# Attention scores in tiles of 64 keys by 72 queries, with TensorE's order written out

## The chip, the cores and the metric

The kernel runs on one core of one Trainium2 chip. The metric is the device time of one execution in microseconds (us). Before the change the median of 10 executions is 1340.0 us (1339.74 to 1340.58).

A core has a matrix engine (TensorE, "PE" in the profile, with its weight loads listed apart as "PEld"), a vector engine (VectorE, "DVE"), a scalar engine that evaluates functions (ScalarE, "ACT"), GpSimd ("POOL") and a queue that issues transfers (SyncE, "SP"). They work at the same time, each on its own list of instructions, and wait for each other through semaphores. A matmul takes its two operands from the on-chip memory SBUF and writes into PSUM, from which ScalarE or VectorE must read the result before the buffer can be used again.

## The reference, cut to what matters

S = 2048 tokens, D = 1024, 32 heads of 32, a window of 8 keys at a distance of 2 tokens, F = 3584:

```python
for layer in range(2):
    # A: sliding, dilated attention
    q, k, v = split_heads(layernorm(layernorm(x)) @ wqkv)
    idx    = pos[:, None] - 2 * arange(8)[None, :]           # each query sees 8 keys
    logits = where(idx >= 0, (q . k[idx]) * 32 ** -0.5, -1e9)
    o      = softmax(logits) . v[idx]
    x      = x + o @ wo
    # B: token-mixing MLP
    h = layernorm(layernorm(x))
    x = x + transpose(gelu(transpose(h) @ w1 + b1) @ w2 + b2)
```

(The doubled layernorm is the call's own and the block's.)

## The kernel before, in words

The tokens are kept in two classes, even (c = 0) and odd (c = 1), because the window steps by two: inside a class of 1024 tokens a query sees its own key and the seven before it. Tokens are taken in blocks of 128, eight to a class.

A layer has these stages, one after another on TensorE: the value projection (`v_proj`, L216); the attention loop; the output projection (`out_proj`, L311), which also adds the residual and makes the next layernorm; the MLP's first product (`gemm1`, L337) and its second (`gemm2`, L380).

**The attention loop** goes over 16 units u = (g, c): a group g of four heads, which fills 128 rows, and a class c. In unit u three kinds of work meet on TensorE:

- *Dense work*: `qk_chunk` (L228) projects q and k of unit u + 1. Unit u + 1 has four chunks (q or k, first or second 512 tokens), each of eight 128x128 by 512 matmuls (L233) into an `m` buffer, of which there are two; VectorE moves each result to SBUF (L236). In a layer's last unit the first four `out_proj` calls stand in their place.
- *Scores*: `scores(u, r)` (L238), three times in a unit, for three, three and two blocks of 128 keys. For each block and each head there is one matmul (L248): 32 rows (the head's own 32 rows of the array), 128 keys as columns, 136 queries streamed. The 136 are the block's own 128 and the 8 that follow, which still see its last keys. The four heads write into four PSUM banks, two `s` buffers of two banks each, all that there are of `s`. ScalarE takes the exponential into `Pm` (L252), VectorE multiplies in place by the 0/1 pattern `band` (L255), in each case once for two heads.
- *Values*: `values(u, b)` (L257), for each half of the class (b = 0, 1): products of `Pm` with v in tiles of 128 rows by 32 columns (L269, L273), sums of `Pm` over keys (L277, L285), all in the one `acc` buffer. ScalarE turns the sums into their reciprocals as exp(-ln) (L288, L289), and VectorE multiplies (L291).

`Pm` exists twice and is used by units in turn. The loop at L434 calls, for each unit: `scores(u, 0)`, chunk, `values(u - 1, 1)`, `scores(u, 1)`, chunk, `scores(u, 2)`, chunk, `values(u, 0)`, chunk.

**What sets the order.** The program names engines and buffers; a planner walks the instructions with a cost model, takes the earliest in the program's order among those that it reckons to be ready, assigns buffers from the pools as they come free, and writes each engine's list with the semaphore waits. So an engine's list is close to the order of the calls but need not be equal to it; where the planner reckons that an operand or a buffer is not there yet, it puts later work ahead. On the chip the list is then run in its order. `rd`, the reciprocals' buffer, has a pool of two; `xr`, `xn`, `xs` and `xo` (rows of the residual stream) share the pool `x2p` of five.

At the start GpSimd makes the constants (the identity, `band`), clears the padding of `qT` (L146) and requests the two bias transfers (L136, L137), whose results VectorE converts (L138, L139), while VectorE also makes the first layernorms (L169 to L177) that the value projection needs.

Of the kernel before, what the change touches and what calls it, by code (L numbers as in the profile page):

```python
# [14 lines left out]
P = 128  # L15
H = 32
DH = 32
# [8 lines left out]
def kernel(  # L26
# [33 lines left out]
    KW = P + W  # L60
    PAD = W
# [13 lines left out]
    x2p = pool("x2p", 5)  # L75
    rdp = pool("rdp", 2)
# [32 lines left out]
    def ln_exp_table():  # L109
# [13 lines left out]
    band = const.tile([P, KW], BF16, name="band")  # L123
    nc.gpsimd.memset(band[:], 1.0)
    nc.gpsimd.affine_select(out=band[:], in_=band[:], compare_op=ALU.is_ge, fill=0.0, base=0,
                            pattern=[[1, KW]], channel_multiplier=-1)
    nc.gpsimd.affine_select(out=band[:], in_=band[:], compare_op=ALU.is_ge, fill=0.0, base=W - 1,
                            pattern=[[-1, KW]], channel_multiplier=1)
# [16 lines left out]
    for t in qT:  # L145
        nc.gpsimd.memset(t[:, S:S + PAD], 0.0)  # L146

# [80 lines left out]
    def qk_chunk(u, wts, part, n):  # L228
        g, c = divmod(u, DIL)
        ps = m_tile()  # L230
        lo = c * SC + n * 512
        for kt in range(KD):
            nc.tensor.matmul(ps[:], lhsT=wts[part][:, kt, (g % 2) * P:(g % 2 + 1) * P], rhs=hT[:, kt, lo:lo + 512],  # L233
                             start=(kt == 0), stop=(kt == KD - 1))
        dst = (qT, kT)[part][g % 2]
        nc.vector.tensor_copy(out=dst[:, lo:lo + 512], in_=ps[:])  # L236

    def scores(u, r):  # L238
        g, c = divmod(u, DIL)
        q, k, pm = qT[g % 2], kT[g % 2], Pm[u % 2]  # L240
        ts = range(3 * r, min(3 * r + 3, NI))
        n = len(ts)
        ss = [s_tile() for _ in range(2)]
        for t in ts:
            lo = c * SC + t * P
            for h in range(HG):
                hp = slice(h * DH, (h + 1) * DH)
                nc.tensor.matmul(ss[h // 2][:, h % 2, (t - ts[0]) * KW:(t - ts[0] + 1) * KW],  # L248
                                 lhsT=k[hp, lo:lo + P], rhs=q[hp, lo:lo + KW], start=True, stop=True)
        for b in range(2):  # L250
            pv = pm[:, 2 * b:2 * b + 2, ts[0]:ts[0] + n, :]
            nc.scalar.activation(out=pv.rearrange("p h t k -> p h (t k)"), in_=ss[b][:, :, 0:n * KW], func=ACT.Exp,  # L252
                                 scale=scale, bias=shift[:])
            mk = band[:].unsqueeze(1).unsqueeze(1).to_broadcast([P, 2, n, KW])
            nc.vector.tensor_tensor(out=pv, in0=pv, in1=mk, op=ALU.mult)  # L255

    def values(u, b, v, oT):  # L257
# [24 lines left out]
        for h in range(HG):  # L282
            hp = slice(h * DH, (h + 1) * DH)
            dst = acc[hp, 1, :].rearrange("p (t q) -> p t q", q=P)[:, o0 // P:o0 // P + ns, 0:W]
            nc.tensor.matmul(dst, lhsT=ones[:], rhs=pm[:, h, s0:s0 + ns, P:KW], start=False, stop=True,  # L285
                             skip_group_check=True)
        rd = rdp.tile([P, 512], FP32, name="rd", tag="rd")
# [3 lines left out]
        nc.vector.tensor_tensor(out=oT[g][:, lo:lo + hb * P], in0=acc[:, 0, :], in1=rd[:], op=ALU.mult)  # L291

# [10 lines left out]
    def out_proj(c, i, oT, wo, res, dst, h2):  # L303
        xr = x2("xr")
        nc.sync.dma_start(out=xr[:], in_=res(c, i))
        xn = x2("xn")
        for n in range(NDC):
            ps = m_tile()
            xs_ = slice(n * 512, (n + 1) * 512)
            for g in range(NG):  # L310
                nc.tensor.matmul(ps[:], lhsT=oT[g][:, cols(c, i)], rhs=wo[n][g // 4][:, g % 4, :],  # L311
                                 start=(g == 0), stop=(g == NG - 1))
# [4 lines left out]
        norm_act(h2[c][i][:], xn[:], mean, rs)  # L317

# [73 lines left out]
    for li in range(2):  # L392
# [41 lines left out]
        for u in range(NU):  # L434
            last = u == NU - 1
            if not last:
                if (u + 1) % (2 * DIL) == 0:
                    wts = load_qk((u + 1) // (2 * DIL))
                fill = [lambda part=part, n=n: qk_chunk(u + 1, wts, part, n) for part, n in chunks]
            else:  # L440
                fill = [lambda i=i: out_proj(0, i, oT, wo, res, xa[li], h2) for i in range(4)]
            if u == NU - 2:
                wo = load_wo()
            scores(u, 0)
            fill[0]()
            if u:
                values(u - 1, 1, v, oT)
            scores(u, 1)
            fill[1]()
            scores(u, 2)  # L450
            fill[2]()
            values(u, 0, v, oT)
            fill[3]()
        values(NU - 1, 1, v, oT)
# [41 lines left out]
```

## Time and profile before

| | |
|---|---|
| median of 10 executions | 1340.0 us |
| the profiled execution's own time | 1339.83 us |
| its span, first to last instruction | 1338.1 us |
| TensorE busy | 1313.1 us, 98% of the span |
| VectorE busy | 428.2 us, 32% |
| ScalarE busy | 407.0 us, 30% |
| GpSimd busy | 4.0 us |
| dense q and k matmuls (L233) | 1024, 247.0 us |
| score matmuls (L248) | 1024, 41.0 us |
| value matmuls (L273) of 136 columns | 768, 22.7 us |
| attention loop, layer 1 | 81.3 to 248.3 us |
| attention loop, layer 2 | 738.8 to 905.8 us |

How to read the rows. In an order of time: start, length, engine, line, operation, output and inputs by the program's names, shape, count of merged instructions, and in brackets the idle time of that engine before the row with what ended it. In groups: line, engine, operation, shape and count, then total busy time and mean nanoseconds of one, then the idle time ahead of them. In windows: the stretch and its length, then busy time and count for PE, PEld, DVE, ACT and POOL, then TensorE's granted clock as a share, the DMA engines' share and GB/s. Matmuls overlap and their ends are modelled, so the distance between starts is the surer measure of what one costs. "m", "s" and "acc" are the three kinds of PSUM buffers.

### The profile page before, as it was taken

The numbers are of one execution on the slowest core, as the hardware profiler recorded it, in microseconds if no ns is written. First come the engines' busy times: TensorE is split into PE (matmuls) and PEld (weight loads), VectorE is DVE, ScalarE is ACT, GpSimd is POOL, SyncE is SP. The second block draws the span as 40 slices with busy tenths as digits, with TensorE's granted clock in tenths as the row PEclk, the third lists the DMA queues.
The fourth block names the chain that finished last, engine by engine and source line by source line (L and its number), as shares of the span: only waits on it lengthen the run. The fifth ranks groups of instructions, "written<-read, shape, count | busy, mean of one in ns | idle before, by whom it ended". The sixth has DMA issues, their size and how long they took to land.

```text
span 1338.1 us, 19150 instructions
## 1 busy us (share of the span) xinstructions
PE 1313.1 (98%) x8352; PEld 590.7 (44%) x8352; DVE 428.2 (32%) x774; ACT 407.0 (30%) x622; POOL 4.0 (0%) x13
## 2 busy tenths in 40 slices
PE   6999999999999999999999999999999999999998
PEld 3444444444444444444444444444444444444443
DVE  6146666960000013233210667678300000011111
ACT  4347766542111110000023677675311111000000
POOL 1000000000000000000000000000000000000000
PEclk8999999999999999999999999999999999999999
DMA  9521110462222226546431101124522221334420
GB/s 251 119 64 33 33 33 28 143 193 79 63 79 77 64 70 163 129 127 182 118 95 47 35 17 33 32 75 154 151 79 79 71 81 56 119 94 124 132 89 32
DMA packets 192195, 121.83 MB, mean 91 GB/s; under 512 B 34416, under 2 KB 173680, under 8 KB 192112
## 3 DMA queue, kind: packets, MB, share of 16 engines
q1 hardware_dynamic: 192000, 120.61, 32.2%
q8 instruction: 65, 1.06, 0.3%
q0 software_dynamic: 112, 0.01, 0.1%
q14 instruction: 18, 0.15, 0.0%
HBM read 96.48 MB, written 16.78 MB: 85 GB/s over the span
## 4 chain that ended last, share of the span: by engine, by line
PE 92%; ACT 6%; DMA 1%; issue 0%; DVE 0%; SPq 0%
PE s L380 14%; PE s L337 14%; PE m L233 13%; PE m L311 8%; PE m L216 8%; PE m L380 7%; PE acc L337 7%; PE m L337 7%; PE acc L380 7%; ACT Pm L252 3%; PE s L248 1%; PE acc L273 1%; ACT rd L289 1%; ACT rd L288 1%; PE acc L277 1%; DMA x<-in_A_x_dram 1%
## 5 line engine op out<-in xcount | busy, mean ns | idle before, releaser
L380 PEld LDWEIGHTS <-w 128*128 128x128 bf16 x1792 | 175.4, 98 | 211.4
L337 PEld LDWEIGHTS <-w 128*128 128x128 bf16 x1792 | 175.3, 98 | 211.5
L233 PE MATMUL m<-hT,wqk 128*128 128x512 bf16 x1024 | 247.0, 381 | 0.0
L337 PE MATMUL s<-h,w 128*128 128x512 bf16 x896 | 202.8, 379 | 0.0
L380 PE MATMUL s<-g,w 128*128 128x512 bf16 x896 | 199.9, 379 | 0.0
L383 DVE SCALAR_TENSOR_TENSOR xo<-s,b_sb,xs 128x512 bf16<-128x512 f32 x32 | 24.0, 750 | 540.7 <-PE s L380 536.5
L252 ACT ACTIVATE Pm<-s,shift 128x816 bf16<-128x816 f32 (+1 forms) x192 | 152.3, 861 | 39.6 <-PE s L248 39.6
L233 PEld LDWEIGHTS <-wqk 128*128 128x128 bf16 x1024 | 90.3, 98 | 109.2 <-issue 6.6
L216 PE MATMUL m<-wv,hT 128*128 128x512 bf16 x512 | 113.9, 385 | 5.5 <-ACT hT L199 5.5
L311 PE MATMUL m<-wo,oT 128*128 128x512 bf16 x512 | 112.2, 379 | 0.0
L255 DVE TENSOR_TENSOR Pm<-Pm,band 128x816 bf16<-128x816 bf16 (+1 forms) x192 | 99.9, 532 | 29.7 <-ACT Pm L252 25.1
L337 PE MATMUL acc<-h,w 128*128 128x512 bf16 x448 | 103.9, 379 | 0.0
L380 PE MATMUL acc<-g,w 128*128 128x512 bf16 x448 | 100.6, 379 | 0.0
L380 PE MATMUL m<-g,w 128*128 128x512 bf16 x448 | 99.3, 379 | 0.0
L337 PE MATMUL m<-h,w 128*128 128x512 bf16 x448 | 99.0, 379 | 0.0
L163 ACT ACTIVATE ln<-mv,eps 128x1 f32<-128x1 f32 x64 | 18.7, 293 | 236.7 <-DVE mv L171 236.5
L344 ACT ACTIVATE g<-s,b_sb 128x1024 bf16<-128x1024 f32 x28 | 31.2, 1114 | 166.9 <-PE s L337 166.9
L216 PEld LDWEIGHTS <-hT 128*128 128x128 bf16 x512 | 50.4, 99 | 67.7 <-ACT hT L199 6.1
L236 DVE CAST qT<-m 128x512 bf16<-128x512 f32 x64 | 44.0, 687 | 100.2 <-PE m L233 100.1
L311 PEld LDWEIGHTS <-oT 128*128 128x128 bf16 x512 | 49.3, 98 | 59.6 <-issue 0.9
L291 DVE TENSOR_TENSOR oT<-acc,rd 128x512 bf16<-128x512 f32 x64 | 44.3, 692 | 59.0 <-ACT rd L289 58.9
L288 ACT ACTIVATE rd<-acc 128x512 f32<-128x512 f32 x64 | 38.2, 597 | 66.6 <-PE acc L285 66.6
(50 smaller groups left out, 585.7 us busy)
## 6 DMA issues: line engine op xcount, KB each, us to landing
w<-in_B_w_dram SPq DMA_DIRECT2D x56, 512.0 KB, 3.7
w<-in_B_w_dram SPq DMA_DIRECT2D x64, 448.0 KB, 4.3
wqk<-in_A_wqkv_dram SPq DMA_DIRECT2D x16, 512.0 KB, 5.4
xa<-xn SPq DMA_DIRECT2D x32, 256.0 KB, 2.1
xs<-xa SPq DMA_DIRECT2D x32, 256.0 KB, 3.0
x<-in_A_x_dram SPq DMA_DIRECT2D x16, 256.0 KB, 6.6
wv<-in_A_wqkv_dram SPq DMA_DIRECT2D x8, 512.0 KB, 5.7
xr<-in_A_x_dram SPq DMA_DIRECT2D x16, 256.0 KB, 3.1
```

The source lines that it names most:

```text
L216: nc.tensor.matmul(ps[:], lhsT=hT[:, kt, cols(c, i)], rhs=wv[n][kt // 4][:, kt % 4, :], start=(kt == 0), stop=(kt == KD - 1))
L233: nc.tensor.matmul(ps[:], lhsT=wts[part][:, kt, (g % 2) * P:(g % 2 + 1) * P], rhs=hT[:, kt, lo:lo + 512], start=(kt == 0), stop=(kt == KD ...
L236: nc.vector.tensor_copy(out=dst[:, lo:lo + 512], in_=ps[:])
L252: nc.scalar.activation(out=pv.rearrange("p h t k -> p h (t k)"), in_=ss[b][:, :, 0:n * KW], func=ACT.Exp, scale=scale, bias=shift[:])
L255: nc.vector.tensor_tensor(out=pv, in0=pv, in1=mk, op=ALU.mult)
L288: nc.scalar.activation(out=rd[:], in_=acc[:, 1, :], func=ACT.Ln)
L291: nc.vector.tensor_tensor(out=oT[g][:, lo:lo + hb * P], in0=acc[:, 0, :], in1=rd[:], op=ALU.mult)
L311: nc.tensor.matmul(ps[:], lhsT=oT[g][:, cols(c, i)], rhs=wo[n][g // 4][:, g % 4, :], start=(g == 0), stop=(g == NG - 1))
L337: nc.tensor.matmul(pairs[fl][0][dc], lhsT=wt[c][:, i, fl * P:(fl + 1) * P], rhs=h2[c][i][:, dc * 512:(dc + 1) * 512], start=(k == 0), stop ...
L344: nc.scalar.activation(out=g[fb][:, fl, :].rearrange("p (n d) -> p n d", n=2), in_=t[:], func=ACT.Gelu_apprx_tanh, bias=b1_sb[:, ft:ft + 1])
L380: nc.tensor.matmul(aps[dc], lhsT=w2t[ft // HF][:, ft % HF, c::DIL], rhs=g[ft // GF][:, ft % GF, dc * 512:(dc + 1) * 512], start=(ft == 0), ...
L383: nc.vector.scalar_tensor_tensor(out=xo[:, dc * 512:(dc + 1) * 512], in0=aps[dc], scalar=b2_sb[:, i, c:c + 1], in1=xs[:, dc * 512:(dc + 1) ...
```

## The change

- *Score tiles.* A block of 128 keys is taken in two halves r of 64 keys. A half is multiplied with its own 64 queries and the 8 after them: 72 columns streamed instead of 136, and an output of 64 PSUM partitions. A matmul is now 32 rows by 64 columns of the array, so that eight places stand side by side instead of four, and there are twice as many score matmuls, each with its own weight load.
- *Exponential and mask.* `scores(u, b)` is called twice in a unit, for four blocks each. ScalarE takes the exponential of the compact form (4 heads x 4 blocks x 72) into a new tile `pc`, two buffers, in two instructions; VectorE multiplies by `band` (now two copies of a 64-row pattern) and writes into the dense `Pm`, once for each half on 64 partitions. The two corners of each `Pm` block that no half writes are cleared once, at the start, by GpSimd.
- *Order.* `in_order` hangs each call's TensorE instructions behind the last matmul of the call before, so the planner cannot change TensorE's order inside the loop. The loop runs over 32 visits (u, b): scores, chunk, the values of the visit before, chunk. The chunks come as q, q, k, k.
- *Copies.* The chunk of the first 512 tokens (n = 0) is moved to SBUF by ScalarE, the other by VectorE.
- *Buffers and transfers.* `rd` moves into `x2p`, which grows to six; `wo` is requested six visits from the end instead of two units from the end.

```diff
-    x2p = pool("x2p", 5)
-    rdp = pool("rdp", 2)
+    x2p = pool("x2p", 6)
+    pcp = pool("pcp", 2)
...
-    band = const.tile([P, KW], BF16, name="band")
+    band = const.tile([P, HW], BF16, name="band")
...
+    for r in range(2):
+        hb_ = band[r * HK:(r + 1) * HK]
+        nc.gpsimd.affine_select(out=hb_, in_=hb_, compare_op=ALU.is_ge, fill=0.0, base=0,
+                                pattern=[[1, HW]], channel_multiplier=-1)
...
+    for t in Pm:
+        nc.gpsimd.memset(t[0:HK, :, :, HW:KW], 0.0)
+        nc.gpsimd.memset(t[HK:P, :, :, 0:HK], 0.0)
...
-        nc.vector.tensor_copy(out=dst[:, lo:lo + 512], in_=ps[:])
+        if n == 0:
+            nc.scalar.copy(out=dst[:, lo:lo + 512], in_=ps[:])
+        else:
+            nc.vector.tensor_copy(out=dst[:, lo:lo + 512], in_=ps[:])
+        return mm
+
+    last_pe = [None]
+
+    def in_order(f, *args):
+        with tc.issue_after(last_pe[0].ins) if last_pe[0] is not None else nullcontext():
+            last_pe[0] = f(*args)
+
+    HB = NI // 2
 
-    def scores(u, r):
+    def scores(u, b):
         g, c = divmod(u, DIL)
         q, k, pm = qT[g % 2], kT[g % 2], Pm[u % 2]
-        ts = range(3 * r, min(3 * r + 3, NI))
-        n = len(ts)
         ss = [s_tile() for _ in range(2)]
-        for t in ts:
-            lo = c * SC + t * P
-            for h in range(HG):
-                hp = slice(h * DH, (h + 1) * DH)
-                nc.tensor.matmul(ss[h // 2][:, h % 2, (t - ts[0]) * KW:(t - ts[0] + 1) * KW],
-                                 lhsT=k[hp, lo:lo + P], rhs=q[hp, lo:lo + KW], start=True, stop=True)
-        for b in range(2):
-            pv = pm[:, 2 * b:2 * b + 2, ts[0]:ts[0] + n, :]
-            nc.scalar.activation(out=pv.rearrange("p h t k -> p h (t k)"), in_=ss[b][:, :, 0:n * KW], func=ACT.Exp,
-                                 scale=scale, bias=shift[:])
-            mk = band[:].unsqueeze(1).unsqueeze(1).to_broadcast([P, 2, n, KW])
-            nc.vector.tensor_tensor(out=pv, in0=pv, in1=mk, op=ALU.mult)
+        for i in range(HB):
+            for r in range(2):
+                lo = c * SC + (b * HB + i) * P + r * HK
+                for h in range(HG):
+                    hp = slice(h * DH, (h + 1) * DH)
+                    mm = nc.tensor.matmul(ss[h // 2][r * HK:(r + 1) * HK, h % 2, i * HW:(i + 1) * HW],
+                                          lhsT=k[hp, lo:lo + HK], rhs=q[hp, lo:lo + HW], start=True, stop=True)
+        pc = pcp.tile([P, HG, HB, HW], BF16, name="pc", tag="pc")
+        for n in range(2):
+            nc.scalar.activation(out=pc[:, 2 * n:2 * n + 2].rearrange("p h t k -> p h (t k)"), in_=ss[n][:, :, 0:HB * HW],
+                                 func=ACT.Exp, scale=scale, bias=shift[:])
+        for r in range(2):
+            rp = slice(r * HK, (r + 1) * HK)
+            mk = band[rp].unsqueeze(1).unsqueeze(1).to_broadcast([HK, HG, HB, HW])
+            nc.vector.tensor_tensor(out=pm[rp, :, b * HB:(b + 1) * HB, r * HK:r * HK + HW], in0=pc[rp], in1=mk, op=ALU.mult)
+        return mm
...
-        rd = rdp.tile([P, 512], FP32, name="rd", tag="rd")
+        rd = x2("rd", [P, 512], FP32)
...
-        chunks = [(0, 0), (1, 0), (0, 1), (1, 1)]
+        chunks = [(0, 0), (0, 1), (1, 0), (1, 1)]
+        last_pe[0] = None
         for part, n in chunks:
-            qk_chunk(0, wts, part, n)
+            in_order(qk_chunk, 0, wts, part, n)
...
+        for vis in range(2 * NU):
+            u, b = divmod(vis, 2)
+            if b == 0 and u + 1 < NU and (u + 1) % (2 * DIL) == 0:
+                wts = load_qk((u + 1) // (2 * DIL))
+            if vis == 2 * NU - 6:
                 wo = load_wo()
-            scores(u, 0)
...
+            in_order(scores, u, b)
+            for n in range(2):
+                if n and vis:
+                    in_order(values, *divmod(vis - 1, 2), v, oT)
+                if u + 1 < NU:
+                    in_order(qk_chunk, u + 1, wts, *chunks[2 * b + n])
+                else:
+                    in_order(out_proj, 0, 2 * b + n, oT, wo, res, xa[li], h2)
+        in_order(values, NU - 1, 1, v, oT)
```

Here P = 128, W = 8, HK = 64, KW = 136 and HW = 72; `values` and `out_proj` now return their last matmul and are otherwise as they were.

More of the change, by code (lines that the diff above doesn't have):

```diff
@@ L60 @@
     KW = P + W
+    HK = P // 2
+    HW = HK + W
     PAD = W
@@ L232, in qk_chunk @@
         for kt in range(KD):
-            nc.tensor.matmul(ps[:], lhsT=wts[part][:, kt, (g % 2) * P:(g % 2 + 1) * P], rhs=hT[:, kt, lo:lo + 512],
-                             start=(kt == 0), stop=(kt == KD - 1))
+            mm = nc.tensor.matmul(ps[:], lhsT=wts[part][:, kt, (g % 2) * P:(g % 2 + 1) * P], rhs=hT[:, kt, lo:lo + 512],
+                                  start=(kt == 0), stop=(kt == KD - 1))
         dst = (qT, kT)[part][g % 2]
-        nc.vector.tensor_copy(out=dst[:, lo:lo + 512], in_=ps[:])
@@ L284, in values @@
             dst = acc[hp, 1, :].rearrange("p (t q) -> p t q", q=P)[:, o0 // P:o0 // P + ns, 0:W]
-            nc.tensor.matmul(dst, lhsT=ones[:], rhs=pm[:, h, s0:s0 + ns, P:KW], start=False, stop=True,
-                             skip_group_check=True)
-        rd = rdp.tile([P, 512], FP32, name="rd", tag="rd")
+            mm = nc.tensor.matmul(dst, lhsT=ones[:], rhs=pm[:, h, s0:s0 + ns, P:KW], start=False, stop=True,
+                                  skip_group_check=True)
+        rd = x2("rd", [P, 512], FP32)
         nc.scalar.activation(out=rd[:], in_=acc[:, 1, :], func=ACT.Ln)
@@ L291, in values @@
         nc.vector.tensor_tensor(out=oT[g][:, lo:lo + hb * P], in0=acc[:, 0, :], in1=rd[:], op=ALU.mult)
+        return mm
     def load_wo():
@@ L310, in out_proj @@
             for g in range(NG):
-                nc.tensor.matmul(ps[:], lhsT=oT[g][:, cols(c, i)], rhs=wo[n][g // 4][:, g % 4, :],
-                                 start=(g == 0), stop=(g == NG - 1))
+                mm = nc.tensor.matmul(ps[:], lhsT=oT[g][:, cols(c, i)], rhs=wo[n][g // 4][:, g % 4, :],
+                                      start=(g == 0), stop=(g == NG - 1))
             nc.vector.tensor_tensor(out=xn[:, xs_], in0=ps[:], in1=xr[:, xs_], op=ALU.add)
@@ L317, in out_proj @@
         norm_act(h2[c][i][:], xn[:], mean, rs)
+        return mm
     order = [(c, i) for c in range(DIL) for i in range(NI)]
```

25 lines of the change are left out of this document (2 added, 23 removed).

## The prediction

> **What bounds the kernel now.** I read the page's engine shares first, then three windows, then one unit of the attention loop in order of time, then single instants of it for start times.
>
> ```profile
> span 1338.1 us, 19150 instructions
> PE 1313.1 (98%) x8352; PEld 590.7 (44%) x8352; DVE 428.2 (32%) x774; ACT 407.0 (30%) x622; POOL 4.0 (0%) x13
> 81.33:90.19 8.86, 8.86 (x90) 3.76 (x90) 6.11 (x11) 6.09 (x8) 0.00 (x0) 1.00 0.01 2
> 100.28:110.37 10.09, 9.79 (x117) 4.29 (x118) 6.91 (x13) 7.10 (x10) 0.00 (x0) 1.00 0.10 32
> ```
>
> The profiled execution took 1339.83 us, 1.73 around its span; the median is 1340.0. TensorE is the bound, at full clock (the 1.00 after the five engines). A unit u takes 10.09 us and, in 100.28 to 110.37, holds 6.91 us of VectorE and 7.10 of ScalarE. Units 1 to 14 of each layer are alike; unit 0 (8.86) lacks one values block, and the last has out_proj in place of the projection. The change touches only these 32 units. One of them, TensorE's rows:
>
> ```profile
> 110.37 0.36 PE L248 MATMUL s<-qT,kT 32*128 32x136 bf16 x12
> 110.66 1.90 PE L233 MATMUL m<-hT,wqk 128*128 128x512 bf16 x8
> 110.77 1.77 ACT L252 ACTIVATE Pm<-s,shift 128x816 bf16<-128x816 f32 x2 [0.83 <-PE s L248]
> ...
> 112.49 0.19 PE L269 MATMUL acc<-Pm,v 128*32 128x8 bf16 x4
> 112.50 0.25 PEld L273 LDWEIGHTS <-v 128*32 128x32 bf16 x16
> 112.53 0.40 PE L273 MATMUL acc<-Pm,v 128*32 128x136 bf16 x16
> ...
> 112.98 0.19 PE L285 MATMUL acc<-Pm,ones 128*32 128x32 bf16 x4
> ...
> 113.10 0.36 PE L248 MATMUL s<-qT,kT 32*128 32x136 bf16 x12
> ...
> 113.39 1.90 PE L233 MATMUL m<-hT,wqk 128*128 128x512 bf16 x8
> ...
> 115.38 0.30 PE L248 MATMUL s<-qT,kT 32*128 32x136 bf16 x4
> ...
> 115.61 0.39 PE L233 MATMUL m<-hT,wqk 128*128 128x512 bf16 x1
> ...
> 116.21 0.29 PE L248 MATMUL s<-qT,kT 32*128 32x136 bf16 x4 [0.21 <-ACT Pm L252]
> ...
> 116.44 1.68 PE L233 MATMUL m<-hT,wqk 128*128 128x512 bf16 x7
> ...
> 118.05 0.42 PE L273 MATMUL acc<-Pm,v 128*32 128x136 bf16 x16
> ...
> 118.63 1.90 PE L233 MATMUL m<-hT,wqk 128*128 128x512 bf16 x8
> ...
> 120.46 0.35 PE L248 MATMUL s<-qT,kT 32*128 32x136 bf16 x10
> ```
>
> A row's length includes the modelled tail of its last matmul, so I go from start to start. A chunk of eight dense matmuls holds the array 110.66 to 112.49 = 1.83 us. Its own pace is (1.90 - 0.39) / 7 = 0.216 each, 1.73 for eight, so leaving a chunk for small tiles costs 0.10. Values take 0.61 (112.49 to 113.10) and 0.58 (118.05 to 118.63). A score piece of twelve takes 0.29 (110.37 to 110.66). The third piece is broken in two around one dense matmul and waits: its chunk began at 113.39 and would end at 115.22, but the scores start at 115.38; the lone matmul from 115.61 would give way at 115.61 + 0.216 + 0.10 = 115.93, but the next start is 116.21. That is 0.16 + 0.28 = 0.44 us of waiting, and the releaser named is the exponential, ACT Pm.
>
> **The change, part by part.** Each unit becomes two visits: scores (S), a chunk, values, a chunk. Dense matmuls, values and the total of dense work stay. So a new unit is 4 x 1.83 + 0.61 + 0.58 + 2 x S = 8.51 + 2 x S, where S runs from the first score matmul to the first dense one.
>
> S is the unknown: 32 pairs of load and matmul, 32 rows by 64 keys by 72 queries, eight places in the array. No row has this shape. The nearest ones (the first is one instant inside the twelve, with the twelfth alone left):
>
> ```profile
> 110.51 0.22 PE L248 MATMUL s<-qT,kT 32*128 32x136 bf16 x1
> ...
> 112.99 0.18 PE L285 MATMUL acc<-Pm,ones 128*32 128x32 bf16 x1
> ```
>
> - Tail: the last score matmul starts at 110.51, dense work at 110.66: 0.15 us with 136 columns. At 0.216 / 512 = 0.42 ns a column, 64 columns fewer are 0.03 less: 0.12.
> - Spread within a round: four L285 in different places start within 0.19 - 0.18 = 0.01 us, about 3.3 ns apart; eight of them 0.025.
> - A round of eight cannot be shorter than its matmul (72 x 0.42 = 0.03) nor, likely, than its load: at 112.50 the loads of 32 columns start and at 112.53 the matmuls that need them. So 0.027 for 32 columns (an estimate, the rows round), 0.055 for 64.
>
> Four rounds are three intervals: 3 x 0.055 + 0.025 + 0.12 = 0.31 us. Low end, loads hidden too: 3 x 0.03 + 0.025 + 0.12 = 0.24. High end, eight places worth no more than the four of today's twelve, which start (0.36 - 0.22) / 11 = 12.7 ns apart: 31 x 0.0127 + 0.12 = 0.51. I take 0.31, since the load is what the row at 112.53 shows waiting.
>
> Then a steady unit is 9.13 instead of 10.09: 0.96 saved, made of 0.44 waiting, one switch out of dense work of five (0.10), and shorter scores. Fourteen give 13.44. Unit 0: 8.86 against 4 x 1.83 + 0.58 + 0.62 = 8.52, saves 0.34. The last unit: score pieces of 0.29 + 0.29 + 0.23 (115.38 to 115.61) become 0.62, saves 0.19. A layer 13.97, two layers 27.9. On the profiled time: 1339.83 - 27.9 = 1311.9, and with the 0.17 between that run and the median, 1312.
>
> **What the other engines get.** They must stay hidden under a visit of 4.57 us.
>
> ```profile
> L252 ACT ACTIVATE Pm<-s,shift 128x816 bf16<-128x816 f32 x128 | 113.1, 933 | 39.0 <-PE s L248 39.0
> L255 DVE TENSOR_TENSOR Pm<-Pm,band 128x816 bf16<-128x816 bf16 x128 | 74.3, 581 | 28.9 <-ACT Pm L252 25.1
> L291 DVE TENSOR_TENSOR oT<-acc,rd 128x512 bf16<-128x512 f32 x64 | 44.3, 692 | 59.0 <-ACT rd L289 58.9
> L236 DVE CAST qT<-m 128x512 bf16<-128x512 f32 x64 | 44.0, 687 | 100.2 <-PE m L233 100.1
> L252 ACT ACTIVATE Pm<-s,shift 128x544 bf16<-128x544 f32 x64 | 42.2, 716 | 0.7 <-PE s L248 0.7
> L289 ACT ACTIVATE rd<-rd 128x512 f32<-128x512 f32 x64 | 40.3, 630 | 2.1
> L288 ACT ACTIVATE rd<-acc 128x512 f32<-128x512 f32 x64 | 38.2, 597 | 66.6 <-PE acc L285 66.6
> L218 ACT CAST v<-m 128x512 bf16<-128x512 f32 x64 | 37.4, 585 | 61.6 <-PE m L216 61.5
> L255 DVE TENSOR_TENSOR Pm<-Pm,band 128x544 bf16<-128x544 bf16 x64 | 27.9, 435 | 0.7
> ```
>
> - Exponentials: (933 - 716) / 272 = 0.80 ns an element; 576 elements cost 742 ns. ScalarE per visit: 2 x 0.742 + a copy of 0.585 + 0.597 + 0.630 = 3.30.
> - Masks: (581 - 435) / 272 = 0.54 ns; 1152 elements on half the partitions cost 0.76. VectorE: 2 x 0.76 + 0.687 + 0.692 = 2.90.
> - Who is late next: the first exponential starts 0.40 after S does (110.77 against 110.37), both end near 1.95, masks at 3.5. The values that need them start in the next visit at 4.57 + 0.31 + 1.83 = 6.71: 3.2 us of slack. If masks ran at half speed (1.4 each) they would end at 4.8, still in time. The s buffers are free from 1.95, the next S asks at 4.57: the 0.44 wait has no heir. The copy that moves to ScalarE comes behind the exponentials and ahead of the logarithm: dense work of the chunk ends at 2.14, so about 2.35 to 2.94, and its buffer is wanted again at 4.88. If this cover went, each late 0.1 us would cost 6.4 us in all (64 visits).
> - rd in the six x2 slots instead of two of its own, wo requested one unit earlier: in the steady loop nothing else takes more than a slot of x2, and wo is needed in the last unit only. Nothing, either way; at worst one out_proj of a layer waits a few tenths.
> - Start-up: four memsets of Pm on GpSimd.
>
> ```profile
> 0.38 0.10 POOL L480 MEMSET const-bfloat16-1.0<- 128x1 bf16 x1
> 0.80 0.20 POOL masks.py:197 MEMSET ident<- 128x128 bf16 x1 [0.29 <-POOLq L480]
> 1.76 1.68 POOL L136 DMA_DIRECT2D b_bf<-in_B_b_dram x1
> 16.40 0.13 DVE L138 CAST b_sb<-b_bf 128x28 f32<-128x28 bf16 x1
> 17.05 0.55 DVE L177 TENSOR_SCALAR x<-x,mv,rs 128x1024 bf16<-128x1024 bf16 x1 [0.44 <-ACT rs L164]
> DMA to landing us min/median/max: 10.2/10.9/11.7
> ```
>
> At (0.20 - 0.10) / 127 = 0.8 ns an element, 2048 elements cost 1.7 us, four 7 us. They stand ahead of the bias transfers, which then leave near 9 and land near 20. If the casts kept their place in VectorE's list at 16.4, the normalization behind them would slip by up to 4 us, and the first value projections with it. The planner places a cast where it reckons its data landed, so I take 0 and keep +4.
>
> **Rivals.**
> 1. The eight places do not overlap as rounds: the two halves of one row group load in turn. Then a round is 0.11 and S = 3 x 0.11 + 0.025 + 0.12 = 0.48, or 0.51 by today's pace: + 0.17 to 0.20 x 64 = 11 to 13, so 1323 to 1325. For it: only column tiles of 32 and row tiles of 128 are in the trace, never both. Against: the four loads of L273 in one set of rows do not queue.
> 2. Slower: each score pair has a fixed price of its own. All 27.9 us are gone when S is longer by 27.9 / 64 = 0.44, at 0.75, which is (0.75 - 0.12) / 31 = 20 ns a pair, since the pairs double from 32 to 64 a unit; a little above it the kernel is slower than before (at 22 ns, 1312 + 64 x 0.49 = 1343). For it: the shape is new and its work per pair is tiny. Against: sixteen L273 in (0.40 - 0.22) / 15 = 12 ns each, and four L285 at 3 ns. The Trainium skill, "TensorE: Matmul & The Clock Gate", section "Wait — 56ns, not 53.3ns?", states that start-to-start never drops below about 25 ns however few columns. By that figure S would be 31 x 0.025 + 0.12 = 0.90 and the time 1349, an estimate from that page. The L273 and L285 rows of this trace are under the figure, though they lie in different places of the array.
> 3. Slower: feeding instructions becomes the bound. Today 116 matmuls and 116 loads go out in 10.09 us, 43 ns each; a new unit has 148 of both. If 43 ns is the limit, it takes 296 x 0.0435 = 12.9 us and the kernel about 1418; it decides from 10.09 / 296 = 34 ns. For it: over a whole unit the trace shows no higher rate. Against: the shown stretch 112.49 to 113.39 sends 80 instructions, 11 ns each.
> 4. The change does not do what it says: the stall is moved. If values or scores waited as long as today (0.44 a unit), 1312 + 0.44 x 28 = 1324.
>
> **How the numbers follow.** Forecast, S from 0.24 to 0.42: 1307 to 1319, chance 0.70. Rivals 1 and 4: 1319 to 1328, 0.17. Between 0.72 and 0.79 of S lies no change: 0.04. Rivals 2 and 3: 0.09. A run of this kernel is told from no change by about 0.2% (2.7 us). Range: the low end of S gives 1312 - 0.07 x 64 = 1307.5, the high end 1312 + 0.20 x 64 = 1325; start-up lies inside. I write 1306 to 1325. Faster 0.87, same 0.04, slower 0.09.
>
> **What would show it right or wrong.** Right: steady units of about 9.1 us; score rows x32 of 32*64 with a dense start some 0.31 after them; no ACT or DVE named before a score or values row; values still 0.6; dense chunks 1.83. S of 0.5 is rival 1, above 0.75 rival 2; loads spaced evenly without a releaser in dense chunks too are rival 3; a releaser before TensorE rows is rival 4. Wrong in another way: a gap before 23 us that today's trace lacks.

## The result, and the profile after

| | before | after |
|---|---|---|
| median, us | 1340.04 (1337.21 to 1340.71, 29 executions) | 1307.81 (1307.03 to 1308.78, 8 executions) |
| profiled execution / its span, us | 1339.83 / 1338.1 | 1308.57 / 1306.9 |
| steady unit, us | 10.09 | 9.05 |
| unit 0 / last unit, us | 8.86 / 16.84 | 8.33 / 16.67 |
| first score matmul of a layer to its last out_proj matmul, us | 208.20 | 192.85 |

The changed kernel takes 0.9761 of the time, 95% interval 0.9753 to 0.977. The forecast was 1312 in a range of 1306 to 1325.

The page of the changed kernel, its head and two groups of the costliest (busy us, mean ns of one, idle time before them), beside the head of before:

```profile
span 1306.9 us, 20991 instructions
...
PE 1290.1 (99%) x9376; PEld 581.4 (44%) x9376; DVE 388.0 (30%) x646; ACT 383.9 (29%) x622; POOL 11.6 (1%) x19
...
L275 DVE TENSOR_TENSOR Pm<-pc,band 64x1152 bf16<-64x1152 bf16 x128 | 96.3, 752 | 65.2 <-ACT pc L270 63.2
...
L270 ACT ACTIVATE pc<-s,shift 128x576 bf16<-128x576 f32 x128 | 87.8, 737 | 59.9 <-PE s L266 59.9
```

TensorE is still the bound, and its busy time fell by 23.0 us although it runs 1024 more matmuls; so part of the 31.3 us of the profiled time was idle before and the larger part was counted as busy. An exponential takes 737 ns (the prediction had 742), a mask 752 (760).

Three stretches of the changed kernel (sum, then busy time of TensorE's matmuls, its loads, VectorE, ScalarE, GpSimd, then the granted clock): a steady unit, the last unit of layer 0, and the loop of layer 0 to the end of its output projection.

```profile
98.13:107.18 9.05, 9.05 (x151) 3.98 (x150) 5.59 (x9) 6.37 (x10) 0.00 (x0) 1.00 0.19 62
215.70:232.37 16.67, 16.61 (x209) 7.57 (x209) 15.13 (x28) 10.18 (x17) 0.00 (x0) 1.00 0.45 142
80.76:273.61 192.85, 192.79 (x2593) 85.68 (x2593) 134.87 (x219) 125.95 (x203) 0.00 (x0) 1.00 0.21 66
```

In the steady unit TensorE is busy for all 9.05 us; the 0.3 us between 9.79 and 10.09 of before are gone. The loop is 208.20 - 192.85 = 15.35 us shorter per layer, and it begins at 80.76 instead of 81.33. Twice 15.35 and 0.57 make 31.3, the whole difference of the profiled times; the stretch between the two loops and the one behind the second are as long as before.

The steady unit in order of time (start, length, engine, line, what, count, idle before):

```profile
98.13 0.34 PE L266 MATMUL s<-qT,kT 32*64 32x72 bf16 x32
...
98.40 1.90 PE L240 MATMUL m<-hT,wqk 128*128 128x512 bf16 x8
98.63 1.37 ACT L270 ACTIVATE pc<-s,shift 128x576 bf16<-128x576 f32 x2 [0.93 <-PE s L266]
100.03 1.54 DVE L275 TENSOR_TENSOR Pm<-pc,band 64x1152 bf16<-64x1152 bf16 x2 [1.01 <-ACT pc L270]
...
100.23 0.19 PE L290 MATMUL acc<-Pm,v 128*32 128x8 bf16 x4
...
100.34 0.59 ACT L244 CAST qT<-m 128x512 bf16<-128x512 f32 x1 [0.34 <-PE m L240]
...
100.84 1.90 PE L240 MATMUL m<-hT,wqk 128*128 128x512 bf16 x8
...
102.27 0.69 DVE L312 TENSOR_TENSOR oT<-acc,rd 128x512 bf16<-128x512 f32 x1 [0.70 <-ACT rd L310]
102.67 0.34 PE L266 MATMUL s<-qT,kT 32*64 32x72 bf16 x32
...
102.94 1.90 PE L240 MATMUL m<-hT,wqk 128*128 128x512 bf16 x8
...
104.77 0.42 PE L294 MATMUL acc<-Pm,v 128*32 128x136 bf16 x16
```

The order is the one written: scores, chunk, values, chunk. All 32 score pairs of a visit stand in one row, with no dense matmul between them, and no TensorE matmul row names a releaser. S, from the first score to the first dense matmul, is 98.40 - 98.13 = 0.27 us. A chunk is still 100.23 - 98.40 = 1.83, values 100.84 - 100.23 = 0.61. The exponentials end 1.87 us after S begins (98.63 + 1.37), the masks 3.44 after it, and the next visit's scores start 4.54 after it.

How the 32 pairs go is seen at one instant just behind them, where the last of them alone is left:

```profile
102.81 0.19 PE L266 MATMUL s<-qT,kT 32*64 32x72 bf16 x1
```

It starts 102.81 - 102.67 = 0.14 us after the first: 31 intervals, about 4.5 ns each on average. Taken apart by such instants, the first round of eight needs 53 ns until the second begins and the later rounds 33 ns. The remaining 0.13 us of S is the tail until dense work starts.

### The profile page after: what moved, and what is told of

It reads as the page before. It is cut to its first block, busy times and chain, and to the rows that moved or that the text cites. A ratio compares the mean times of both kernels' runs of the same rounds, so it can differ in the third digit from the quotient of the medians.

```text
span 1306.9 us, 20991 instructions
## 1 busy us (share of the span) xinstructions
PE 1290.1 (99%) x9376; PEld 581.4 (44%) x9376; DVE 388.0 (30%) x646; ACT 383.9 (29%) x622; POOL 11.6 (1%) x19
## 4 chain that ended last, share of the span: by engine, by line
PE 97%; DVE 1%; DMA 1%; ACT 0%; issue 0%; SPq 0%
PE m L240 18%; PE s L403 15%; PE s L360 15%; PE m L223 9%; PE m L403 7%; PE m L360 7%; PE acc L360 7%; PE acc L403 7%; PE m L333 7%; PE acc L294 1%; PE s L266 1%; PE acc L298 1%; DMA wv<-in_A_wqkv_dram 0%; DMA x<-in_A_x_dram 0%; DVE xn L335 0%; DVE bn L176 0%
## 5 line engine op out<-in xcount | busy, mean ns | idle before, releaser
L240 PE MATMUL m<-hT,wqk 128*128 128x512 bf16 x1024 | 241.8, 380 | 0.0
L275 DVE TENSOR_TENSOR Pm<-pc,band 64x1152 bf16<-64x1152 bf16 x128 | 96.3, 752 | 65.2 <-ACT pc L270 63.2
L270 ACT ACTIVATE pc<-s,shift 128x576 bf16<-128x576 f32 x128 | 87.8, 737 | 59.9 <-PE s L266 59.9
L225 ACT CAST v<-m 128x512 bf16<-128x512 f32 x64 | 37.4, 584 | 65.6 <-PE m L223 65.6
L246 DVE CAST qT<-m 128x512 bf16<-128x512 f32 x32 | 21.8, 681 | 95.3 <-PE m L240 95.3
```

What stands on the lines that cost most here:

```text
L225: nc.scalar.copy(out=v[c][i][:, n * 512:(n + 1) * 512], in_=ps[:])
L240: mm = nc.tensor.matmul(ps[:], lhsT=wts[part][:, kt, (g % 2) * P:(g % 2 + 1) * P], rhs=hT[:, kt, lo:lo + 512], start=(kt == 0), stop=(kt = ...
L270: nc.scalar.activation(out=pc[:, 2 * n:2 * n + 2].rearrange("p h t k -> p h (t k)"), in_=ss[n][:, :, 0:HB * HW], func=ACT.Exp, scale=scale ...
L275: nc.vector.tensor_tensor(out=pm[rp, :, b * HB:(b + 1) * HB, r * HK:r * HK + HW], in0=pc[rp], in1=mk, op=ALU.mult)
```

## The experiments

Each is a variant of the kernel before or of the changed one; ratios are to the kernel before, with 95% intervals; waits are given as total us, times, longest us. The theory: the gain is the stall of the third score piece (0.44 us a unit), one switch out of dense work less, and shorter scores; the small tiles matter chiefly since they make two pieces possible. The rivals: the written order does it; or the tiles by themselves do.

**The order alone: old tiles, three pieces, every call of the loop (scores, values, chunks and output projections) tied to the one before.**

```diff
-            scores(u, 0)
+            in_order(scores, u, 0)
...
-                values(u - 1, 1, v, oT)
+                in_order(values, u - 1, 1, v, oT)
```

> The kernel before with its old tiles and its three score pieces, and only TensorE's order written out (each call's matmuls behind the call before). My theory: the order as such saves nothing. The third piece is no longer split around one dense matmul, which spares a switch and a second start, some 0.2 us a unit, but it then stands whole behind the second exponential of the piece before, which ends near 116.2 in the profile of before while the piece could start at 115.2: about 1.0 us of waiting instead of 0.44. Unit about 10.4 us, kernel 1345 to 1350. Rival (the written order is what made the gain): unit 9.1 to 9.5 us, kernel 1310 to 1325.

Measured 1346.32 us, ratio 1.0046 (1.0031 to 1.0061): slower by 6 us, as expected. A steady unit of this variant, around the third score piece, and the total of its waits beside that of before:

```profile
105.98 0.29 PE L255 MATMUL s<-qT,kT 32*128 32x136 bf16 x4
106.81 0.30 PE L255 MATMUL s<-qT,kT 32*128 32x136 bf16 x4 [0.54 <-ACT Pm L259]
```

```profile
PE s L255 <- ACT Pm L259: 15.0, 28, 0.5
```

```profile
PE s L248 <- ACT Pm L252: 6.0, 28, 0.2
```

The wait for the exponentials is the same one, 28 times in either kernel. The planner had hidden part of it by slipping one dense matmul into the broken piece; with the order tied, TensorE stands idle for 0.54 us instead of 0.21. The old order written out is a loss. In the changed kernel the ties move nothing: without them the planner writes the same list, instruction by instruction, for every engine. What is new there is the order of the calls, not that it is enforced.

**The tiles alone: small tiles, exponentials in compact form and masks into zeroed `Pm`, but three pieces (3, 3 and 2 blocks), the planner's order and copies on VectorE.**

```diff
-    def scores(u, r):
+    def scores(u, j):
...
+        t0, t1 = 3 * j, min(3 * j + 3, NI)
...
+                    nc.tensor.matmul(ss[h // 2][r * HK:(r + 1) * HK, h % 2, i * HW:(i + 1) * HW],
+                                     lhsT=k[hp, lo:lo + HK], rhs=q[hp, lo:lo + HW], start=True, stop=True)
```

> The kernel before with the new score tiles, the compact exponential and the mask by halves, but in three pieces a unit as before, the planner's order, copies on VectorE. My theory: the small tiles themselves are worth little on TensorE (pieces of 24, 24 and 16 pairs at 0.24, 0.24 and 0.20 us by the pace seen in the changed kernel, against 0.29, 0.29 and 0.46), and most of the gain comes from two pieces instead of three, with a whole visit between them. The third piece still waits for the exponentials of the second, about 0.5 us. Unit about 9.7 us, kernel about 1327 (1322 to 1332). Rival (tile shape carries the gain): unit 9.1 us, kernel 1308 to 1313.

Measured 1328.89, ratio 0.9916 (0.9901 to 0.993): a third of the whole gain, inside the expected range. Its third and first piece in a steady unit:

```profile
103.53 0.22 PE L256 MATMUL s<-qT,kT 32*64 32x72 bf16 x2
...
103.93 0.26 PE L256 MATMUL s<-qT,kT 32*64 32x72 bf16 x14 [0.19 <-ACT pc L260]
...
104.13 1.90 PE L240 MATMUL m<-hT,wqk 128*128 128x512 bf16 x8
...
108.37 0.30 PE L256 MATMUL s<-qT,kT 32*64 32x72 bf16 x24
108.61 0.60 PE L240 MATMUL m<-hT,wqk 128*128 128x512 bf16 x2
```

A piece of 24 pairs takes 0.24 (108.37 to 108.61) where twelve old ones took 0.29; the stall remains, 103.53 to 104.13 = 0.60 for a piece worth 0.20. So a steady unit divides as follows (dense 4 x 1.83 = 7.32 and values 1.19 in each):

| | scores | waiting | extra switch | unit |
|---|---|---|---|---|
| before | 1.04 | 0.44 | 0.10 | 10.09 |
| small tiles, three pieces | 0.68 | 0.40 | none | 9.59 |
| changed kernel | 0.54 | none | none | 9.05 |

The step from three pieces to two is worth 0.54 of the 1.04. It cannot be made with the old tiles: four blocks of 136 queries are 544 columns for a head, and its half of an `s` buffer holds 512; four of 72 are 288. In the whole kernel the variant gains 11 us and not the 14 that 0.50 in each of 28 steady units would make; in its last units the output projections wait:

```profile
PE m L321 <- DVE xn L323: 4.5, 4, 1.8
```

The changed kernel has no such wait. Two things stay open: an order of the old tiles with more work ahead of the third piece was not run, so it is not shown that only smaller tiles can lose the wait; and the new order of the chunks and the earlier request of `wo` were not run apart.

**The moved copies: all of them on VectorE again.**

```diff
-        if n == 0:
-            nc.scalar.copy(out=dst[:, lo:lo + 512], in_=ps[:])
-        else:
-            nc.vector.tensor_copy(out=dst[:, lo:lo + 512], in_=ps[:])
+        nc.vector.tensor_copy(out=dst[:, lo:lo + 512], in_=ps[:])
```

> The changed kernel with all q and k copies on VectorE as before. My theory: both engines have slack in a visit of 4.53 us (VectorE would have 3.6 us of work), so nothing moves: 1308, within 1.5 us. Rival (the move of copies to ScalarE was needed to keep the PSUM buffers free in time): waits of chunks on VectorE copies, 1312 or more.

Measured 1308.23, ratio 0.9761 (0.9745 to 0.9777): no difference. The copies are not what the unit waits for, on either engine.

**Values right behind the scores, then both chunks.** One switch out of dense work less in each visit.

```diff
-            for n in range(2):
-                if n and vis:
-                    in_order(values, *divmod(vis - 1, 2), v, oT)
+            if vis:
+                in_order(values, *divmod(vis - 1, 2), v, oT)
+            for n in range(2):
```

> The changed kernel with the values of the visit before called right behind the scores, both ahead of the two chunks, so that dense work is left once a visit instead of twice. My theory: each time dense work gives way costs 0.10 us, and nothing else is on the path: 64 x 0.10 = 6.4 us less, 1301 to 1302, visits of about 4.43 us. Rival (values and scores must stand apart, since ScalarE's logarithm and exponentials then come at once and the next visit waits for PSUM or masks): no gain or a loss, 1308 or more, with ScalarE or VectorE named ahead of TensorE rows.

Measured 1312.54 (1309.30 to 1314.07), ratio 0.9791 (0.9776 to 0.9806): a miss. The steady visits did take 4.40 and 4.43 instead of 4.51 and 4.54. But the visit that begins the last unit took 11.74 instead of 7.99. There, in order of time, and in the waits:

```profile
217.04 0.69 DVE L335 TENSOR_TENSOR xn<-m,xr 128x512 bf16<-128x512 f32 x1 [1.61 <-DMA xr<-in_A_x_dram]
217.78 5.30 PE L333 MATMUL m<-wo,oT 128*128 128x512 bf16 x16 [2.02 <-DVE xn L335]
```

```profile
PE m L333 <- DVE xn L335: 9.0, 6, 2.9
```

Two output projections now follow each other, each with a residual block to fetch; the transfer comes late, VectorE's add waits for it, and with the two `m` buffers full TensorE waits 9.0 us in six places of the two layers. In the changed kernel no such row is among the waits.

**The same, except in the last unit.**

```diff
+            inner = u + 1 < NU
             for n in range(2):
-                if n and vis:
+                if n == (0 if inner else 1) and vis:
```

> As the run with values right behind the scores, but in the last unit of a layer values stand between two output projections, as in the changed kernel. Theory: the loss of the former run lies in the last unit alone, where its visit took 11.75 us instead of 7.99 and the output projection waited for rows of x; the steady visits were 0.11 us shorter as forecast. So 58 visits x 0.11 = 6.4 us less than the changed kernel: 1301 to 1302. Rival (the adjacency itself upsets what follows the loop, by moving buffers or transfers): 1308 or more.

Measured 1301.91, ratio 0.9716 (0.9702 to 0.9731): as expected, 5.9 us under the changed kernel. A visit of this variant:

```profile
101.95 0.34 PE L266 MATMUL s<-qT,kT 32*64 32x72 bf16 x32
102.22 0.42 PE L294 MATMUL acc<-Pm,v 128*32 128x136 bf16 x16
...
102.80 3.63 PE L240 MATMUL m<-hT,wqk 128*128 128x512 bf16 x16
106.35 0.34 PE L266 MATMUL s<-qT,kT 32*64 32x72 bf16 x32
```

Sixteen dense matmuls run on for 106.35 - 102.80 = 3.55 us where two chunks of 1.83 took 3.66. That is the price of a switch out of dense work measured directly: 0.11 us, against 0.10 worked out before. Setting scores and values a chunk apart thus costs 0.11 us a visit; that part of the new order is not what makes the changed kernel faster.

**What a score pair costs: every pair twice.** The output is unchanged, since each product is only written again.

```diff
+        for rep in range(2):
             for i in range(HB):
```

> The changed kernel with every score matmul and its weight load made twice in a row of 64 pairs instead of 32 (the same results land in the same place). It measures what 32 more pairs cost. Theory: TensorE takes pairs at the 3.3 ns seen in the changed kernel's score rows, so S grows by 32 x 3.3 = 0.106 us, the kernel by 64 x 0.106 = 6.8 us to 1314 or 1315. Rival 2 of the prediction (a fixed price per pair, some 20 ns): S grows by 0.64 us, the kernel by 41 us. Rival 3 (instructions come no faster than a limit near today's): a visit has 212 instead of 148 instructions, and dense chunks become longer too, well above 1.83 us. Rounds paced by weight loads (0.055 us each): 14 us more, 1322.

Measured 1335.62, ratio 0.9967 (0.9954 to 0.998). No theory had this. A visit, then two stretches cut out of it, from before the first pair to just before the 33rd matmul and behind it:

```profile
104.49 0.60 PEld L267 LDWEIGHTS <-kT 32*64 32x64 bf16 x64 [0.42 <-issue]
104.50 0.71 PE L267 MATMUL s<-qT,kT 32*64 32x72 bf16 x64
105.14 0.55 PEld L240 LDWEIGHTS <-wqk 128*128 128x128 bf16 x4
```

```profile
104.50 0.34 PE L267 MATMUL s<-qT,kT 32*64 32x72 bf16 x32
```

```profile
104.74 0.47 PE L267 MATMUL s<-qT,kT 32*64 32x72 bf16 x32
```

The first 32 matmuls go as before, their last starting 0.14 us after the first. Then nothing starts for 0.10 us; the second 32 begin at 104.74, and dense work follows at 105.14, after 0.40 us. By single instants these start every 8.3 ns, which is 4.2 ns for each of the two instructions of a pair. A visit becomes 4.88 or 4.91, 0.38 longer: 24 us for 64 visits. The output projections now wait for `xn` as well, which makes the rest of the 28 us:

```profile
PE m L334 <- DVE xn L336: 3.7, 4, 1.2
```

Two readings: TensorE holds about 64 instructions ahead, filled while the dense matmuls run, and beyond them it is fed at a lower rate; or writing a place a second time is what costs. The next run tells them apart.

**Each half of the pairs twice.** The break should stay at the 33rd pair if it counts instructions, and move to the 17th if repetition makes it.

```diff
-        for rep in range(2):
-            for i in range(HB):
+        for half in range(2):
+            for rep in range(2):
+                for i in range(2 * half, 2 * half + 2):
```

> As the run with every score pair made twice, which cost 0.43 us a visit and not 0.11: there 32 pairs went at 3.3 ns, then came 100 ns of nothing and 32 more at 8.3 ns. Here the 64 pairs are in another order: the first 16 pairs, the same 16 again, the last 16, those again. Theory A (a store of instructions that is full after dense work holds 32 pairs and is then refilled at 4.2 ns an instruction): the break stays at the 33rd pair, visits of about 4.97 us and a kernel of 1335. Theory B (writing the same place again makes TensorE wait): breaks come at the 17th and the 49th pair, where a repetition begins, and the 33rd has none; some 0.1 us more a visit, 1341 or another time off 1335.

Measured 1335.27, ratio 0.9966 (0.9952 to 0.998); visits of 4.88 and 4.91 (4.97 came from spreading all of the former run's loss over the visits). A visit, cut ahead of its 33rd matmul and behind it:

```profile
88.71 0.34 PE L268 MATMUL s<-qT,kT 32*64 32x72 bf16 x32
```

```profile
88.95 0.47 PE L268 MATMUL s<-qT,kT 32*64 32x72 bf16 x32
```

The break of 0.10 us stands before the 33rd pair again, as in all 64 visits of either run, and no wait of that size comes at the 17th or the 49th. So repetition does not make it, and it goes by what has gone out since dense work. Whether that is 64 instructions, 32 loads, 32 matmuls or the 0.14 us they take was not told apart; a store of 64 instructions is a reading that fits, and the cause of the 0.10 us stays open. The Trainium skill, "TensorE: Matmul & The Clock Gate", section "Architectural detail: the array is 16× 32×32, not 1× 128×128", gives TensorE's queue a depth of 64; the break after 32 pairs agrees with it.

**The start: `Pm` cleared by VectorE, so that GpSimd requests the biases early again.**

```diff
-        nc.gpsimd.memset(t[0:HK, :, :, HW:KW], 0.0)
-        nc.gpsimd.memset(t[HK:P, :, :, 0:HK], 0.0)
+        nc.vector.memset(t[0:HK, :, :, HW:KW], 0.0)
+        nc.vector.memset(t[HK:P, :, :, 0:HK], 0.0)
```

> The changed kernel with the four memsets of Pm on VectorE instead of GpSimd, and the bias transfers requested right away again as in the kernel before. Theory: in the changed kernel GpSimd's memsets put the bias transfers off to 9.98 us, and so the third block of x lands at 10.3 instead of 13.7 us; that is worth about 0.6 us net at the loop's start, after the first two normalizations lost 1.7 us beside the memsets. With the bias transfers early again, x lands late again and the loop starts near 81.3 or a little later: kernel 1308.4, within 1 us. Rival (the late bias transfers have nothing to do with it, the memsets on GpSimd are pure cost): loop starts at 80 or earlier, 1306 to 1307.

Measured 1309.24, ratio 0.977 (0.9756 to 0.9785). The time lies where the theory had it, within 1 us of 1308.4; the loop begins at 80.61, which is neither the 81.3 of the theory nor the 80 of its rival. The run decides nothing, because the beginning scatters: in the profiles of the changed kernel and of the six variants above that keep its start, the loop begins between 79.42 and 80.76, and in those of the two kernels with the old start at 81.33 and 81.81. The new start is the earlier one in each of these, but by how much it gains, and why, is not shown.

**The start and the order together: values next to scores but for the last unit, `Pm` cleared by VectorE, biases requested only once the last x block (`after`) has landed, and converted by GpSimd.**

```diff
+        nc.gpsimd.tensor_copy(out=b1_bf[:, 0:1], in_=after)
+        nc.gpsimd.tensor_copy(out=b2_bf[:, 0, 0:1], in_=after)
...
-        nc.vector.tensor_copy(out=b1_sb[:], in_=b1_bf[:])
+        nc.gpsimd.tensor_copy(out=b1_sb[:], in_=b1_bf[:])
```

> As the run before, with the start changed too: Pm is cleared by VectorE, and GpSimd requests the bias transfers only once the last block of x has landed, and converts the biases itself. Theory of the start: both of what slowed it are gone (the element-wise bias transfers among the first loads of x, GpSimd's memsets beside VectorE's first normalizations), so the value projection starts earlier and the loop 1 to 4 us sooner: 1298 to 1301. Rival (the start hangs on the transposing transfers of later blocks): no change against the run before, 1301 to 1302.

Measured 1300.37, ratio 0.9704 (0.9688 to 0.972): the fastest of all, below both kernels; none of its executions (1299.31 to 1301.02) is as slow as the fastest of the variant without the new start (1301.65). Its loop begins at 78.53, against 80.47 there and 79.42 at the earliest in the seven profiles named above. What the transfers of the first 25 us moved, in 40 slices of 0.625 us (GB/s), in the kernel before, in the changed kernel and in this variant, with the row of the variant's first bias request:

```profile
GB/s 0 0 7 295 298 193 193 324 367 351 364 383 181 62 70 64 74 137 146 325 341 334 359 367 382 375 393 380 387 387 380 400 383 380 397 379 337 306 310 301
```

```profile
GB/s 0 0 10 216 246 297 236 224 264 293 370 356 382 369 369 354 362 364 359 367 382 375 397 383 276 66 70 46 70 91 108 302 400 390 387 390 358 333 320 305
```

```profile
GB/s 0 0 3 252 220 236 226 352 370 351 349 369 339 306 333 349 369 365 375 375 379 397 380 383 393 383 397 380 383 393 380 356 324 297 289 290 290 248 66 175
```

```profile
21.98 1.81 POOL L142 DMA_DIRECT2D b_bf<-in_B_b_dram  x1 [0.27 <-POOL b_bf L140]
```

In the changed kernel the rate falls to between 46 and 108 GB/s for six slices, from 15.6 to 19.4 us, while the biases requested at 9.98 and 11.66 are on their way (they land near 20). In the kernel before, which requests them at 1.76 and 3.70, the hollow lies at 8.1 to 11.9, with 62 to 146 GB/s. In this variant it is gone from its old place and comes later, as 40 slices of 0.75 us from 15 to 45 us show:

```profile
GB/s 391 388 388 385 391 383 344 304 294 288 287 193 73 265 212 10 38 33 5 35 41 47 18 98 87 251 312 299 280 270 103 270 201 262 311 134 287 203 76 264
```

From 26.3 to 32.3 us the rate is between 5 and 47. The trace's packets agree: 78 of the 112 packets of the bias transfers start in the changed kernel's hollow, and 87 of 112 in this late one. In the changed kernel's hollow the other queue starts 155 packets, which take 388 ns each on average; this variant starts 805 in the same stretch, at 79 ns. So the hollow goes with the bias transfers in three placements; how they slow the others was not looked into, and in the late stretch transposing transfers run beside them. The loop begins 1.9 us earlier than in the variant without the new start, and the median is 1.5 us lower. How much of this is the biases, how much the clearing on VectorE and how much the conversion on GpSimd, all changed in this run, is not separated.

## Why the prediction was right, point by point

- **Right: the bound and the sum.** The unit became 4 x 1.83 + 0.61 + 0.58 + 2 x S, with chunks and values unchanged. The measured 9.05 is 8.51 + 0.54.
- **Right: the 0.44 of waiting is gone and has no heir.** No TensorE matmul in the steady unit names ScalarE or VectorE; the run with three pieces of the same tiles keeps 0.40 of it. Rival 4 (the stall moved, 1324) is out: in the changed kernel's loop no TensorE row is among the waits.
- **A term mis-sized: S, 0.27 instead of 0.31.** The tail was right (0.13 against 0.12). The rounds were not: "a round of eight cannot be shorter than its matmul (72 x 0.42 = 0.03) nor, likely, than its load" set the pace by the load, 0.055, and the later rounds take 33 ns. Three intervals and the spread of the last round were put at 0.19 and measured 0.14. Two S a unit in 28 steady units are 28 x 0.08 = 2.2 us. The first interval of 53 ns is near 0.055 by chance: the eight matmuls of the first round start within 24 ns, and the second round's first load starts at 102.695, only 26 ns ahead of its matmul at 102.721. So a load of 64 columns held its matmul up no longer than the 0.027 us that the prediction read for 32 columns; doubling it was the step that failed. The later loads go out between the matmuls of the round before. The prediction's own row at 110.51 spoke against the load as the pace: twelve old pairs, three rounds of four with 128 columns each, start within 0.14 us, about 0.07 a round, where 0.027 for 32 columns would make 0.11 a round. What fits both is the other term, the columns streamed (72 x 0.42 = 30 ns beside 33, 136 x 0.42 = 57 ns beside 63 and 69), which the prediction kept for its low end; no run varied the columns alone.
- **A term missed: unit 0.** It saved 0.53, not 0.34. Of the difference, 0.08 is S; the other 0.10 is a switch: the first visit has no values, so its two chunks run as one of sixteen. The rule of 0.10 for each switch was in the prediction and was not applied there. Both layers: 0.4 us. The last unit saved 0.17, against 0.19.
- **A term missed: the start**, taken as 0, was -0.57 in the two profiles compared. The feared slip of the normalization did not come: the casts were put at 20.89 in VectorE's list, behind the landing of the biases. Nor did the gap before 23 us: the waits ahead of TensorE's rows there are 12.6 us in all, against 12.7 before. With a scatter of 1.3 us between profiles of the same start, the size of this term is luck.
- **How far off in all.** These three, 2.2 + 0.4 + 0.6, are 3.2 of the 3.3 us between the forecast for the profiled execution, 1311.9, and its 1308.57. They have one sign, so nothing cancelled: the mechanism carried the forecast. The median of the other executions is 0.8 us lower still, and 1307.81 lies only 1.8 us above the lower end of the range.
- **Right: copies, `rd`, masks and exponentials cost nothing in the steady unit.** The copies were tried alone and made no difference; the masks end 3.44 us into a visit, against the forecast 3.5. The rest was not tried alone; no TensorE row waits for it.
- **Rival 1** (half-row loads in turn, S of 0.48 or more) is out by S.
- **Rival 2** (20 ns a pair): the pairs of one visit start 4.5 ns apart on average. The figure that the prediction cites from the Trainium skill, "TensorE: Matmul & The Clock Gate", section "Wait — 56ns, not 53.3ns?", about 25 ns from start to start, would have made 0.78 us of the 0.14. It does not hold here from one place of the array to the next; in the same place the starts are 33 ns apart or more.
- **Rival 3** (the feed of instructions) is out for this kernel, but it is no phantom. The doubled pairs went at 4.2 ns an instruction behind the 64th, far from the 34 ns at which it would have decided. The changed kernel's bursts are 32 pairs: just as many as go without the break.

## What to carry to other kernels

A smaller tile can be worth more by what fits into a buffer than by its own speed: here half of a steady unit's gain came from one piece fewer, and with it a wait that disappeared. Price the switches of TensorE between dense and small work (0.10 to 0.11 us each here), look at the first and the last pass of a loop on their own, and keep a burst of small load-and-matmul pairs within what goes out without a break (32 here). When two steps with transfers of their own are put side by side, ask whether the second's data are there. Before a difference at a kernel's start is explained, compare the start in profiles of variants that leave it alone (1.3 us of scatter here).

## What was not expected of the hardware

- Pairs of load and matmul in eight places of the array start at 33 ns a round of eight, about 4 ns a pair, behind a first round of 53 ns; after 32 pairs comes a break of 0.10 us and then a pace of 8.3 ns a pair.
- VectorE's normalization does not end before a GpSimd memset that runs beside it. The changed kernel's start, in order of time:

```profile
6.21 1.80 POOL L152 MEMSET Pm<- 64x2048 bf16 x1
6.82 1.46 DVE L184 TENSOR_SCALAR x<-x,mv,rs 128x1024 bf16<-128x1024 bf16 x1
...
8.04 1.99 POOL L153 MEMSET Pm<- 64x2048 bf16 x1
...
9.00 1.31 DVE L184 TENSOR_SCALAR x<-x,mv,rs 128x1024 bf16<-128x1024 bf16 x1 [0.60 <-ACT rs L171]
...
12.87 0.55 DVE L184 TENSOR_SCALAR x<-x,mv,rs 128x1024 bf16<-128x1024 bf16 x1
```

  The normalization takes 0.55 us alone, 1.46 and 1.31 beside a memset, and ends 0.27 or 0.28 us after the memset both times (8.28 against 8.01, 10.31 against 10.03). Not every VectorE instruction is held: the statistics at 6.14 take 0.64 us beside the first of these memsets, and 0.64 at 12.19 without one. The Trainium skill, "SBUF — State Buffer", section "🔬 SBUF: two separate sides", calls the ports that VectorE and GpSimd share an exclusive lock, held for a whole instruction, against VectorE instructions in a two-port mode and some others; the two ends agree with a lock, and in which mode the normalization ran is not shown. The prediction had counted the memsets only as a delay on GpSimd's own list. What this cost the start was not measured apart.
- For 3.8 us of the time that the two bias transfers (7 and 4 KB) are in flight, the core's transfers as a whole fall from about 370 to between 46 and 108 GB/s.
